# Some key blocks' exponentials moved from ScalarE to VectorE in a two-branch attention kernel

## The chip, the cores and the metric

One NeuronCore of one Trainium2 chip (trn2). The metric is the device time of one execution in microseconds (us), the median over several executions. Runs of one kernel mostly agree within 0.3%. The profile is that of one execution. PE is the matrix engine, PEld its weight loads, ACT is ScalarE, DVE is VectorE, POOL is GpSimd.

## The reference, cut to what matters

```python
def reference(A_x, A_wqkv, A_wo, B_x, B_wqkv, B_wo, gate_w):   # S = 2048 tokens, D = 640, bf16
    x = A_x
    g = sigmoid((x * gate_w).sum(-1, keepdims=True))
    a = A_ref(x, A_wqkv, A_wo)     # full softmax attention, 32 heads of 20
    b = B_ref(x, B_wqkv, B_wo)     # each query sees 8 keys, 2 apart; 32 heads of 20
    return g * a + (1 - g) * b
```

Branch A needs 32 x 2048 x 2048 exponentials. In the kernel that is 2048 *units* of 128 keys x 512 queries (4 query chunks x 8 groups of four heads x 16 key blocks x 4 heads). A *quad* is the four heads of one key block: 4 units.

## The kernel before

The program's order is made when it is built: Python generators ask for tasks, and a small scheduler with a time for each task decides what each engine's queue gets next. ACT computes the exponentials in tiles of 3 and 2 units in turn. PE makes the scores of the next tile, adds the products with the values (`pv`), and does "side" work in what is left: projections, branch B, and the fold (output projection of a finished query chunk). When it has nothing to do it issues filler matmuls that keep it busy. All side work goes through two PSUM banks, `side[0]` and `side[1]`.

```python
mmc = lambda n: max(n, 64) / 2400.0 + 0.004       # the scheduler's times, us
dvc = lambda n, mode=1: 0.10 + n * 1.0417e-3 / mode
actc = lambda n: 0.08 + n * 0.8334e-3

def exp(s):
    u0, n = tiles[s]
    exps[s] = T("act", actc(512 * n), lambda e: e.activation(
        ebuf[s % NE][:, 0:512 * n], score[s % 2][:, 0:512 * n], ACTF.Exp, scale=SCALE),
      reads=[("score", s % 2)], writes=[("ebuf", s % NE)])

def filler(limit):
    while sch.avail["pe"] + 0.32 <= limit and sch.load(2.3) < FILL:
        ...   # a matmul into a free side bank (ident), or into the output bank with zero weights

def gen_fold(qc):                 # output projection of query chunk qc
    while not (done.get(("b", 2 * qc + 1)) and all(done.get(("norm", qc * NQ + q)) for q in range(NQ))):
        yield ("cond",)
    ...                           # 13 accumulating matmuls for each block of 128 tokens

# in the main loop, when a group g of four heads is finished:
if g >= NSLOT:                    # NSLOT output slots, 12 here
    run_until(("fold", (g - NSLOT) // NQ))
```

`gen_bproj` and `gen_b` are branch B: projections and window sums on PE, products on DVE, for 8 blocks of 256 tokens. They and the fold yield `("pe", ...)`, that is, they get PE only where a matmul fits before the next scores are due.

Of the kernel before, what the change touches and what calls it, by code (L numbers as in the profile page):

```python
# [8 lines left out]
U16 = mybir.dt.uint16  # L9
ALU = mybir.AluOpType  # L10
# [18 lines left out]
TOK = 256  # L29

# [195 lines left out]
def _build(ctx, nc, A_x, A_wqkv, A_wo, B_wqkv, B_wo, gate_w, out):  # L226
# [22 lines left out]
    qT = [sb([P, 512], BF16, "qT%d" % i) for i in range(3)]  # L249
    ebuf = [sb([P, 512 * TSZ[i % 2]], BF16, "ebuf%d" % i) for i in range(NE)]  # L250
    NSLOT = 12
    oTn = sb([P, NSLOT, 512], BF16, "oTn")
    oTt = sb([P, 512], FP32, "oTt")
    oNt = sb([P, 512], BF16, "oNt")
# [4 lines left out]
    gB = [sb([P, 512], FP32, "gB%d" % i) for i in range(2)]  # L259
    gwT = sb([P, CN], BF16, "gwT")  # L260
    gwrep = sb([P, CN, P], BF16, "gwrep")
# [15 lines left out]
    repB = [sb([P, 2 * TOK], BF16, "repB%d" % i) for i in range(4)]  # L277
# [7 lines left out]
    Sel = sb([P, 32], BF16, "Sel")  # L285
# [42 lines left out]
    T("dve", 0.06, lambda e: e.memset(warm[:, :], 0.0), writes=["warm"])  # L328
    T("act", 1.4, lambda e: e.activation(warm[:, 2:4], warm[:, 0:2], ACTF.Exp), reads=["warm"], writes=["warm2"])
# [24 lines left out]

    def constants():
# [10 lines left out]
        T("dve", 0.15, lambda e: e.tensor_copy(Sel[:, :], Rep[:, 0:32]), reads=["Rep"], writes=["Sel"])  # L366
# [63 lines left out]
    done = {}  # L430

# [23 lines left out]
    def gen_q(g):  # L455
        qc, q = divmod(g, NQ)
        sl = g % 3
        while not done.get(("k", q)):
# [12 lines left out]
                            mmc(512), first=False)  # L471
        yield ("dve",)
        t = T("dve", dvc(512), lambda e: e.tensor_copy(qT[sl][:, :], side[b][:, :]),  # L473
              reads=[("side", b)], writes=[("qT", sl)])
# [16 lines left out]

    def gen_gate(qc):
        while qc > 1 and not done.get(("fold", qc - 2)):
            yield ("cond",)
        b = yield from bank()
        mms = [(side[b][:, :], gwrep[:, c, :], xT[:, c, qc * 512:(qc + 1) * 512]) for c in range(CN)]
        yield from mm_group(b, mms, ["gwrep"] + XT(qc), mmc(512))
        yield ("act", sch.ready(("side", b)))
        t = T("act", actc(512), lambda e: e.activation(gtan[:, :], side[b][:, :], ACTF.Tanh, scale=0.5),
              reads=[("side", b)], writes=["gtan"])  # L500
        release(b, t)
        yield ("dve",)
        T("dve", dvc(512, 2), lambda e: e.tensor_scalar(gB[qc % 2][:, :], gtan[:, :], -0.5, 0.5, op0=ALU.mult, op1=ALU.add),
          reads=["gtan"], writes=[("gB", qc % 2)])
        yield ("dve",)
        T("dve", dvc(512), lambda e: e.transpose(gtr[:, :], gtan[:, :]), reads=["gtan"], writes=["gtr"])
        T("dve", 0.1, lambda e: e.tensor_scalar(gA[qc % 2][:, :], gtr[:, 0:512:32], 0.5, 0.5, op0=ALU.mult, op1=ALU.add),
          reads=["gtr"], writes=[("gA", qc % 2)])
        done[("gate", qc)] = True

    def gen_norm(g):
# [3 lines left out]
        while not done.get(("gate", qc)):  # L515
# [7 lines left out]
        oo = _ap(oNt, 0, [[32, 16], [1, 32]])  # L523
        ii = _ap(oTt, 0, [[32, 16], [1, 32]])
        T("dve", dvc(512), lambda e: e.tensor_tensor(oo, ii, ib, ALU.mult), reads=["rcp", "oTt"],
          writes=["oNt"])
        yield ("dve",)
        T("dve", dvc(512), lambda e: e.transpose(oTn[:, sl, :], oNt[:, :]), reads=["oNt"],
          writes=[("oTn", sl)])
        done[("norm", g)] = True  # L530

# [10 lines left out]

    def gen_bproj(u):
# [4 lines left out]
        for m in range(3):  # L548
            while m == 2 and u > 0 and not done.get(("bp", u - 1)):
                yield ("cond",)  # L550
            if u > 0 and m > 0:
                bb, key = ((kB, "kB"), (vB, "vB"))[m - 1]
                T("dve", 0.15, lambda e, bb=bb: e.tensor_copy(bb[:, :, 0:PADB], bb[:, :, TOK:TOK + PADB]), reads=[key], writes=[key])
            for f0 in range(0, CN, 2):
# [12 lines left out]
                t = T("dve", dvc(n * TOK), lambda e, o=o, i=i: e.tensor_copy(o, i), reads=[("side", b)], writes=[key])  # L567
# [5 lines left out]
    def gen_b(u):  # L573
        qc, hu = divmod(u, 2)
        while not (done.get(("bqk", u)) and done.get(("gate", qc)) and (u == 0 or done.get(("b", u - 1)))):
            yield ("cond",)

        b = yield from bank()
        for half in range(2):
            for w4 in range(4):  # L580
                w = half * 4 + w4
                yield ("dve",)
                ks = kB[:, :, PADB - DIL * w:PADB - DIL * w + TOK]
                T("dve", dvc(CN * TOK, 2), lambda e, w=w, ks=ks: e.tensor_tensor(prodB(w), qB[:, :, :], ks, ALU.mult),  # L584
                  reads=["qB", "kB"], writes=[("prod", w)] + (["stage"] if u == 0 else []))
            for f in range(CN):
                yield ("pe", 0.11, sch.ready(*[("prod", half * 4 + w4) for w4 in range(4)]))

                def fn(e, f=f, half=half, b=b):
                    ins = None  # L590
                    for w4 in range(4):
                        w = half * 4 + w4
                        pr = _ap(stage, (w * CN + f) * TOK, [[1, TOK]])
                        ins = e.matmul(side[b][32 * w4:32 * w4 + 32, half * TOK:(half + 1) * TOK], Sel[:, :], pr,  # L594
# [4 lines left out]
                T("pe", 0.11, fn, reads=[("prod", half * 4 + w4) for w4 in range(4)] + ["Sel"], mode="col",  # L599
                  **({"writes": [("side", b)]} if (half == 0 and f == 0) else {"accum": [("side", b)]}))  # L600
        done[("bl", u)] = True
        if u == 0:
# [6 lines left out]
        T("dve", dvc(TOK), lambda e, b=b: e.tensor_copy(mB[:, :], side[b][:, 0:TOK]), reads=[("side", b)], writes=["mB"])  # L609
        T("dve", dvc(TOK), lambda e, b=b: e.tensor_tensor(mB[:, :], side[b][:, TOK:2 * TOK], mB[:, :], ALU.max),  # L610
          reads=[("side", b), "mB"], writes=["mB"])
        yield ("dve",)
        T("dve", 0.2, lambda e: e.tensor_copy(cB[0:64, :], mB[64:128, :]), reads=["mB"], writes=["cB"])
        T("dve", 0.25, lambda e: e.tensor_tensor(mB[0:64, :], mB[0:64, :], cB[0:64, :], ALU.max),
          reads=["mB", "cB"], writes=["mB"])
        T("dve", 0.2, lambda e: e.tensor_copy(cB[0:32, :], mB[32:64, :]), reads=["mB"], writes=["cB"])
        T("dve", 0.25, lambda e: e.tensor_tensor(mB[0:32, :], mB[0:32, :], cB[0:32, :], ALU.max),
# [10 lines left out]

        b = yield from bank()
        mms = [(side[b][:, 0:TOK], Rep[:, :], eB[:, hh * TOK:(hh + 1) * TOK]) for hh in range(2)]  # L630
        yield from mm_group(b, mms, ["Rep", "eB"], mmc(TOK), per=2)
        yield ("dve",)
        t = T("dve", TOK * 7.5e-3, lambda e, b=b: e.reciprocal(rB[:, :], side[b][:, 0:TOK]), reads=[("side", b)], writes=["rB"])
        release(b, t)
        T("dve", dvc(TOK), lambda e: e.tensor_tensor(rB[:, :], rB[:, :], gB[qc % 2][:, hu * TOK:(hu + 1) * TOK], ALU.mult),
          reads=["rB", ("gB", qc % 2)], writes=["rB"])
# [3 lines left out]
        for w4 in range(4):  # L640
# [6 lines left out]
            t = T("dve", dvc(512), lambda e, w4=w4, b=b: e.tensor_copy(repB[w4][:, :], side[b][:, :]),  # L647
                  reads=[("side", b)], writes=[("repB", w4)])
            release(b, t)
            for hh in range(2):  # L650
                w = 4 * hh + w4
                yield ("dve",)
                vs = vB[:, :, PADB - DIL * w:PADB - DIL * w + TOK]
                rr = _ap(repB[w4], hh * TOK, [[0, CN], [1, TOK]])
                T("dve", dvc(CN * TOK, 2), lambda e, w=w, vs=vs, rr=rr: e.tensor_tensor(prodB(w), vs, rr, ALU.mult),  # L655
                  reads=["vB", ("repB", w4)], writes=[("prod", w)])
        done[("bp", u)] = True
        for f0 in range(0, CN, 2):
# [9 lines left out]
            t = T("dve", dvc(n * TOK), lambda e, o=o, i0=i0, i1=i1: e.tensor_tensor(o, i0, i1, ALU.mult),  # L668
# [15 lines left out]
    def gen_prefold():  # L684
# [5 lines left out]
        for i in range(3):  # L690
# [9 lines left out]
            release(b, t)  # L700
        for blk in range(2):
# [79 lines left out]
    DVE_AHEAD = 0.9  # L781

    def step(ent, limit, force):
# [7 lines left out]
        elif req[0] == "dve":  # L791
            if not force and sch.avail["dve"] > now + DVE_AHEAD:
                return False
# [29 lines left out]
    def run_until(flag):  # L823
        n = 0
        while not done.get(flag):
            if not any(step(ent, 1e9, True) for ent in list(gens)):
# [84 lines left out]
    t = T("dve", dvc(512), lambda e: e.tensor_copy(qT[0][:, :], side[1][:, :]), reads=[("side", 1)], writes=[("qT", 0)])  # L911
    bank_free[0] = bank_free[1] = t.end + LAT["dve"]
    done[("k", 0)] = done[("q", 0)] = True
    T("dve", 0.5, lambda e: e.tensor_copy(gwrep[:, :, :], _ap(gwT, 0, [[1, CN], [0, P]])), reads=["gwT"], writes=["gwrep"])
# [4 lines left out]
    NU = QCN * NQ * KBN * 4  # L919
    NG = QCN * NQ  # L920
    tiles = []
    u = 0
    while u < NU:
        n = min(TSZ[len(tiles) % 2], NU - u)
        tiles.append((u, n))
        u += n
    NT = len(tiles)
    exps = {}
    tile_of = {}
    for s, (u0, n) in enumerate(tiles):  # L930
        for i in range(n):
            tile_of[u0 + i] = (s, i)

    def qk(s):
        u0, n = tiles[s]
        sc = score[s % 2]

        def fn(e):
            ins = None
            for i in range(n):  # L940
                g, r = divmod(u0 + i, 64)
                kb, j = divmod(r, 4)
                q = g % NQ
                ins = e.matmul(sc[:, i * 512:(i + 1) * 512], kT[32 * j:32 * j + 32, q, kb * P:(kb + 1) * P],  # L944
                               qT[g % 3][32 * j:32 * j + 32, :], start=True, stop=True)
# [3 lines left out]
        for i in range(n):  # L949
            g, r = divmod(u0 + i, 64)  # L950
            rd.add(("kT", g % NQ, r // 16))
            rd.add(("qT", g % 3))
        T("pe", 0.215, fn, reads=sorted(rd, key=str), writes=[("score", s % 2)], mode="row")

    def exp(s):
        u0, n = tiles[s]
        exps[s] = T("act", actc(512 * n), lambda e: e.activation(  # L957
            ebuf[s % NE][:, 0:512 * n], score[s % 2][:, 0:512 * n], ACTF.Exp, scale=SCALE),
          reads=[("score", s % 2)], writes=[("ebuf", s % NE)])

    def pv(units):
        def fn(e):
            ins = None
            for uu in units:
                g, r = divmod(uu, 64)
                kb, j = divmod(r, 4)
                s, i = tile_of[uu]
# [34 lines left out]
    for s in range(NT + 8):  # L1002
        if next_pv >= NU:
            break
# [88 lines left out]
```

## Time and profile before

| | before |
|---|---|
| median time | 974.33 us before the prediction (973.93 with one run more) |
| ACT busy | 945.8 us of 971.4 |
| of it attention exponentials | 930.1 us, 819 tiles, 2048 units: 0.454 us a unit |
| PE busy | 949.5 us, of it fillers 128.1 + 69.1 = 197 us |
| DVE busy | 433.7 us |

The page's first part and its costliest groups. Columns of a group: line, engine, operation, out<-in, shapes, count; busy us, mean ns of one record; idle time before it and who ended it. "+1 forms" means that the group mixes the named shape with one more, and that the mean is over both.

```profile
PE 949.5 (98%) x6989; PEld 326.8 (34%) x6989; DVE 433.7 (45%) x799; ACT 945.8 (97%) x846; POOL 20.3 (2%) x20
...
L957 ACT ACTIVATE ebuf<-score 128x1536 bf16<-128x1536 f32 (+1 forms) x819 | 930.1, 1434 | 5.6 <-PE score L944 5.6
...
L987 PE MATMUL side<-xT,ident 128*128 128x512 bf16 x457 | 128.1, 382 | 0.0
...
L991 PE MATMUL obank<-xT,zero 128*128 128x512 bf16 x232 | 69.1, 383 | 0.0
```

ACT waits 5.6 us for scores in the whole run, so it is the bottleneck. PE only looks as full: the last two lines are fillers. The waits, longest first, say the same from PE's side: it waits for the exponentials.

```profile
PEld score L944 <- ACT ebuf L957: 234.5, 704, 1.2
```

Two groups by form show what a small operand does to one ACT instruction. Both read 512 columns of PSUM; L735 is a plain copy, L870 adds a bias that it reads from a 128x1 tile (`onesrow`).

```profile
L870 ACT ACTIVATE kT<-side,onesrow 128x512 bf16<-128x512 f32 x4 | 2.8, 688 | 6.9 <-DVE kmx L867 5.4 <-PE score L841 1.5
...
L735 ACT ACTIVATE stage<-side 128x512 bf16<-128x512 f32 x2 | 1.1, 594 | 3.9 <-PE side L716 3.9
```

Last, the busy times of 350 to 850 us, the stretch in which branch B and the folds run: all engines, then the two fillers alone.

```profile
350.00:850.00 500.00, 495.52 (x3793) 172.89 (x3791) 237.57 (x422) 500.00 (x448) 0.00 (x0) 1.00 0.02 5
...
350.00:850.00 500.00, 42.88 (x152) 12.37 (x152) 1.00 0.02 5
...
350.00:850.00 500.00, 44.42 (x150) 11.99 (x150) 1.00 0.02 5
```

The columns of the first line are PE, PEld, DVE, ACT, POOL, then clock, DMA share and GB/s; the other two have PE and PEld only. PE's fillers are 42.9 + 44.4 = 87 us of 500 here: 17% of PE is free, while DVE is free for more than half of the stretch.

### The profile page before, as it was taken

How to read it: one execution, taken by the hardware profiler on the slowest of the kernel's cores; microseconds unless marked ns; L12 is line 12 of the kernel's file. 1: busy time of each engine (PE TensorE's matmuls, PEld its weight loads, DVE VectorE, ACT ScalarE, POOL GpSimd, SP SyncE). 2: the span in 40 equal slices, each digit the busy share in tenths (PEclk: the TensorE clock that was granted, in tenths of full speed). 3: DMA queues.
4: the chain of work that ended last, by engine and by line, in shares of the span. 5: the costliest groups of instructions: out<-in, count | busy, mean ns of one | idle time of the engine just before them, and what ended most of it. 6: DMA issues, size and time to landing. Idle time of an engine off the chain costs nothing.

```text
span 971.4 us, 16623 instructions
## 1 busy us (share of the span) xinstructions
PE 949.5 (98%) x6989; PEld 326.8 (34%) x6989; DVE 433.7 (45%) x799; ACT 945.8 (97%) x846; POOL 20.3 (2%) x20
## 2 busy tenths in 40 slices
PE   7989999999999999999999999999999999999997
PEld 4323323223333333333333333334333332333223
DVE  4654434443555722564653364664512556201112
ACT  4989999999999999999999999999999999999996
POOL 0000000007000000000000000000000000000000
PEclk9999999999999999999999999999999999999999
DMA  6110000020000000000000000000000000000000
GB/s 218 26 43 1 1 1 1 13 91 1 1 1 2 1 1 15 15 1 1 1 1 9 20 2 1 1 1 1 2 1 15 14 2 1 1 1 2 1 1 28
DMA packets 9767, 13.05 MB, mean 13 GB/s; under 512 B 2397, under 2 KB 8413, under 8 KB 9693
## 3 DMA queue, kind: packets, MB, share of 16 engines
q1 hardware_dynamic: 9692, 12.00, 3.7%
q8 instruction: 54, 0.88, 0.4%
q14 instruction: 21, 0.16, 0.1%
HBM read 9.38 MB, written 2.62 MB: 12 GB/s over the span
## 4 chain that ended last, share of the span: by engine, by line
PE 61%; ACT 29%; issue 8%; DVE 1%; DMA 0%; DVEq 0%; ACTq 0%
ACT ebuf L957 28%; PE side L420 19%; PE score L944 17%; PE side L987 10%; PE obank L968 10%; PE obank L991 3%; PE side L859 1%; ACT eB L625 1%; PE score L841 1%; DMA oTn<-in_A_x_dram 0%; PE side L643 0%; PE side L594 0%; ACT xT L850 0%; ACT kT L870 0%; PE score L877 0%
## 5 line engine op out<-in xcount | busy, mean ns | idle before, releaser
L957 ACT ACTIVATE ebuf<-score 128x1536 bf16<-128x1536 f32 (+1 forms) x819 | 930.1, 1434 | 5.6 <-PE score L944 5.6
L944 PE MATMUL score<-qT,kT 32*128 32x512 bf16 x2048 | 319.8, 384 | 9.5 <-ACT ebuf L957 4.7
L968 PE MATMUL obank<-ebuf,vA 128*21 128x512 bf16 x2048 | 184.2, 385 | 0.0
L944 PEld LDWEIGHTS score<-qT,kT 32*128 32x128 bf16 x2048 | 78.3, 91 | 256.3 <-ACT ebuf L957 234.5
L420 PE MATMUL side<-xT,kvw 128*128 128x256 bf16 (+1 forms) x740 | 134.8, 295 | 0.0
L987 PE MATMUL side<-xT,ident 128*128 128x512 bf16 x457 | 128.1, 382 | 0.0
L420 PEld LDWEIGHTS side<-xT,kvw 128*128 128x128 bf16 x740 | 59.6, 97 | 58.7 <-issue 42.0
L968 PEld LDWEIGHTS obank<-ebuf,vA 128*21 128x21 bf16 x2048 | 41.6, 89 | 93.4 <-issue 92.1
L991 PE MATMUL obank<-xT,zero 128*128 128x512 bf16 x232 | 69.1, 383 | 0.0
L467 DVE TENSOR_SCALAR qabs<-side 128x512 uint16<-128x512 uint16 x31 | 21.0, 676 | 89.5 <-PE side L420 89.3
L987 PEld LDWEIGHTS side<-xT,ident 128*128 128x128 bf16 x457 | 37.1, 97 | 59.0 <-issue 30.0
L514 DVE STREAM_TRANSPOSE oTt<-obank 128x512 f32<-128x512 f32 x32 | 22.9, 715 | 70.7 <-PE obank L968 70.7
L655 DVE TENSOR_TENSOR stage<-vB,repB 128x1280 bf16<-128x1280 bf16 x64 | 50.1, 822 | 1.1
L584 DVE TENSOR_TENSOR stage<-qB,kB 128x1280 bf16<-128x1280 bf16 x64 | 49.1, 820 | 0.3
L420 PE MATMUL side<-woA_r,oTn 128*128 128x512 bf16 (+1 forms) x248 | 48.2, 302 | 0.0
L420 PE MATMUL side<-stage,ident 128*128 128x512 bf16 (+1 forms) x192 | 48.1, 347 | 0.0
L444 DVE TENSOR_SCALAR kT<-side,onesrow 128x512 bf16<-128x512 f32 x28 | 20.7, 741 | 61.2 <-PE side L420 61.2
L420 PE MATMUL side<-xT,WqP 128*128 128x512 bf16 x155 | 46.6, 384 | 0.8 <-DVE kT L444 0.8
L761 DVE CAST outsb<-side 128x512 bf16<-128x512 f32 (+1 forms) x24 | 11.8, 490 | 75.8 <-PE side L420 75.8
L668 DVE TENSOR_TENSOR oB<-side,rB 128x512 bf16<-128x512 f32 (+1 forms) x24 | 14.5, 603 | 67.7 <-PE side L420 67.7
L420 PE MATMUL side<-woBp,oB 128*128 128x512 bf16 (+1 forms) x160 | 32.5, 302 | 0.0
L473 DVE CAST qT<-side 128x512 bf16<-128x512 f32 x31 | 21.1, 681 | 19.5 <-PE side L420 19.5
(117 smaller groups left out, 500.4 us busy)
## 6 DMA issues: line engine op xcount, KB each, us to landing
stage<-in_B_wqkv_dram SPq DMA_DIRECT2D x1, 2400.0 KB, 8.6
out_dram<-outsb SPq DMA_DIRECT2D x12, 160.0 KB, 1.8
stage<-in_A_wqkv_dram SPq DMA_DIRECT2D x1, 1600.0 KB, 11.0
oTn<-in_A_x_dram SPq DMA_DIRECT2D x2, 640.0 KB, 5.4
kvw<-in_A_wqkv_dram SPq DMA_DIRECT2D x1, 800.0 KB, 8.4
woA_r<-in_A_wo_dram SPq DMA_DIRECT2D x4, 200.0 KB
woBp<-in_B_wo_dram SPq DMA_DIRECT2D x5, 160.0 KB
oB<-in_A_x_dram SPq DMA_DIRECT2D x1, 640.0 KB, 6.9
```

The lines of the kernel that those rows point to most:

```text
L420: ins = e.matmul(o, l, r, start=(first and i == 0), stop=(last and i == n - 1), skip_group_check=True)
L444: t = T("dve", dvc(512), lambda e, b=b, tcc=tcc: e.tensor_scalar(kT[:, q, tcc * 512:(tcc + 1) * 512], side[b][:, :], onesrow[:, 0:1], None ...
L467: T("dve", dvc(512), lambda e: e.tensor_scalar(qabs[:, :].bitcast(U16), side[b][:, :].bitcast(U16)[:, 1:1024:2], 0x7FFF, None, op0=ALU.bit ...
L473: t = T("dve", dvc(512), lambda e: e.tensor_copy(qT[sl][:, :], side[b][:, :]), reads=[("side", b)], writes=[("qT", sl)])
L514: T("dve", dvc(512), lambda e: e.transpose(oTt[:, :], obank[:, :]), reads=["obank"], writes=["oTt"])
L584: T("dve", dvc(CN * TOK, 2), lambda e, w=w, ks=ks: e.tensor_tensor(prodB(w), qB[:, :, :], ks, ALU.mult), reads=["qB", "kB"], writes=[("pro ...
L655: T("dve", dvc(CN * TOK, 2), lambda e, w=w, vs=vs, rr=rr: e.tensor_tensor(prodB(w), vs, rr, ALU.mult), reads=["vB", ("repB", w4)], writes= ...
L944: ins = e.matmul(sc[:, i * 512:(i + 1) * 512], kT[32 * j:32 * j + 32, q, kb * P:(kb + 1) * P], qT[g % 3][32 * j:32 * j + 32, :], start=Tru ...
L957: exps[s] = T("act", actc(512 * n), lambda e: e.activation(ebuf[s % NE][:, 0:512 * n], score[s % 2][:, 0:512 * n], ACTF.Exp, scale=SCALE), ...
L968: ins = e.matmul(obank[32 * j:32 * j + DV, :], vA[:, kb, g % NQ, j, :], ebuf[s % NE][:, i * 512:(i + 1) * 512], start=(kb == 0), stop=(kb ...
L987: t = T("pe", 0.215, lambda e, b=b: e.matmul(side[b][:, :], ident[:, :], xT[:, 0, 0:512], start=True, stop=True), reads=["ident", ("xT", 0 ...
L991: T("pe", 0.215, lambda e: e.matmul(obank[:, :], zero[:, :], xT[:, 0, 0:512], start=False, stop=False, skip_group_check=True), reads=["zer ...
```

## The change

Its intent: ACT is full and VectorE is half idle, so some quads are taken from the end of a group's key blocks and their exponentials are made on VectorE. The queries are scaled by 128/ln 2 and offset so that a score *is*, in effect, the bit pattern of a bf16 power of two; a clamp and a cubic in the fraction then give the exponential in four VectorE passes. The scores of such a unit ride along in a PE row group that a tile's visit leaves free. The gate is computed by block and some buffers are shared, to make room in memory, and the output has 16 slots in place of 12.

```diff
-    qT = [sb([P, 512], BF16, "qT%d" % i) for i in range(3)]
+    qT = [sb([P, 512], BF16, "qT%d" % i) for i in range(2)]
-    NSLOT = 12
+    NSLOT = 16
+    ebias = sb([P, 1], FP32, "ebias")
+    T("dve", 0.06, lambda e: e.memset(ebias[:, :], -127.0 * LN2), writes=["ebias"])
...
-      t = T("dve", dvc(512), lambda e: e.tensor_copy(qT[sl][:, :], side[b][:, :]),
+      t = T("dve", dvc(512), lambda e: e.tensor_scalar(qT[sl][:, :], side[b][:, :], OCT, offs[:, 0:1], op0=ALU.mult, op1=ALU.add),
...
+    def gen_d(w):                       # two of these workers
+        while True:
+            while lock[w] or not wanted():
+                yield ("cond",)
+            b = yield from bank()       # a side bank, until the clamp has read it
+            it = yield ("ride", b)      # scores made beside those of a tile
+            T("dve", dvc(512), ... tensor_scalar(xD[w], side[b], 16384.0, None, op0=ALU.max))
+            release(b, t)
+            nn = xD[w][:, :].bitcast(U16)[:, 0:1024:2]     # the fraction: low half of the fp32 word
+            T("dve", dvc(512), ... scalar_tensor_tensor(tD, nn, -OCT16, nn, op0=ALU.add, op1=ALU.mult))
+            T("dve", dvc(512), ... scalar_tensor_tensor(tD, nn, H1, tD, op0=ALU.add, op1=ALU.mult))
+            T("dve", dvc(512), ... scalar_tensor_tensor(eD as int16, tD, H2, xD[w], op0=ALU.mult, op1=ALU.add))
...
+    BT0 = 230.0
+    BT1 = 910.0
+    BALL = 208.0
+    def d_time():                       # is a new quad allowed?
+        now = sch.avail["pe"]
+        return now >= D0 and sch.avail["dve"] <= now - DIDLE and bdone[0] >= (now - BT0) / (BT1 - BT0) * BALL
...
     def exp(s):
         exps[s] = T("act", actc(512 * n), lambda e: e.activation(
-            ebuf[s % NE][:, 0:512 * n], score[s % 2][:, 0:512 * n], ACTF.Exp, scale=SCALE),
-          reads=[("score", s % 2)], writes=[("ebuf", s % NE)])
+            ebuf[s % NE][:, 0:512 * n], score[s % 2][:, 0:512 * n], ACTF.Exp, scale=LN2 / 128.0, bias=ebias[:, 0:1]),
+          reads=[("score", s % 2), "ebias"], writes=[("ebuf", s % NE)])
```

The tiles that stay on ACT now need a bias, and it is given as a 128x1 tile. And `bdone`, VectorE's work for branch B as the scheduler has booked it, must keep up with a straight line in time, or no new quad is taken. (I call this the pacing rule.)

## The prediction

> **What bounds the kernel now.** ScalarE. The first part of the page has it busy 945.8 of 971.4 us; the groups of instructions give 930.1 us of that to the attention exponentials (819 tiles, 2048 units of 128x512, so 0.454 us a unit). From 100 to 950 us the stretches show it at 50.0 of every 50 us. The waits agree: the weight loads for scores wait 234.5 us for the exponentials, the exponentials only 5.6 us for scores. PE looks 98% busy, but 197 us of it are fillers (128.1 into the side banks, 69.1 into the output bank). VectorE is busy 433.7 us, so some 540 us are free.
>
> **What the change removes.** Each quad (four heads of one key block) moved to VectorE takes 4 x 0.454 = 1.82 us off ScalarE. The scores of these units ride in free row groups, so PE saves a little.
>
> **What it adds on VectorE.** Four full-width passes a unit: one clamp out of PSUM and three dependent fp32 passes. In the trace a 512-wide pass takes 0.69 us; in a row it starts 0.61 us after the one before if independent, and about 0.73 us if it waits for it. That is about 2.8 us a unit, 11 us a quad (estimate). From 100 to 900 us VectorE has about 435 us to spare; one quad is open at a time, banks and the pace kept for branch B cost some of it. I expect 30 quads (24 to 38), 120 units, so ScalarE loses 120 x 0.454 = 54 us. The gate by unit, the slots, the shared buffers move only a few us, off the critical path.
>
> **What it adds on ScalarE, and decides.** The exponential's bias was zero, an immediate; it becomes a 128x1 operand in memory. The Trainium skill ("ScalarE: Activation LUTs", What ACT_TABLE_LOAD costs) says that each such operand adds about 93 ns to an ACTIVATE. The trace agrees for single instructions: copies of 512 columns without one took 594 ns, the key copy with a bias operand 688 ns. In a stream, exponentials now end 1.344 and 0.916 us apart, only 64 ns over their columns' time. Whether the operand's fetch hides there no record shows directly. But one key copy with a bias was followed by a copy whose data were ready, which started 586 ns later, 159 ns over its columns' time, where plain ones start 51 to 67 ns over[...]. So I think it does not hide (62%): 770 tiles x 80 to 93 ns give back 62 to 72 us, more than 30 quads save.
>
> **Time.** Not hidden: 974 - 54 + 65 = 985 with 30 quads, about 970 with 38. Hidden: 974 - 54 = about 920. All of it is on the critical path. I name 968, between the two and nearer the likelier.
>
> **What would show it.** The ends of neighbouring 1536- and 1024-column exponentials: 1.34/0.92 us if hidden, 1.43/1.00 if not. Their number: near 770. VectorE's busy time: near 750 us. Waits of exponentials for scores: still a few us; if tens of us, VectorE or the banks hold PE up. Fillers: fewer than 197 us.
>
> **What would make it wrong.** Far fewer or more quads; strided reads of 16-bit halves slower than 0.69 us a pass; output products that wait for late quads and stall scores behind them on PE; the bias fetch hidden under the tile before (then over 5% faster).
>
> The chances: faster by over 2% 0.40, within 2% 0.50, slower by over 2% 0.10. Predicted 968 us, 908 to 992.

## The result and the profile after

The change gave 1017.52 us (1016.92 to 1017.77, 4 runs) against 973.93 us. A ratio here is the mean time of one kernel's fast runs over that of the other's of the same rounds, so not quite the ratio of the medians quoted: 1.0453, 95% interval 1.0433 to 1.0474. It is 4.5% slower, outside the predicted range. Executions over 1.5% slower than the fastest of the same kernel are left out of the means.

The page's first part and the exponentials of the kernel after:

```profile
PE 922.8 (91%) x6808; PEld 316.5 (31%) x6915; DVE 615.1 (61%) x1067; ACT 985.6 (97%) x827; POOL 22.9 (2%) x20
...
L1135 ACT ACTIVATE ebuf<-score,ebias 128x1536 bf16<-128x1536 f32 (+1 forms) x792 | 971.3, 1592 | 10.8 <-PE score L1121 10.3
```

There are fewer tiles (792 for 819), and they take more time in all (971.3 for 930.1 us). Busy time for a tile went from 930.1/819 = 1.136 us to 971.3/792 = 1.226 us. ACT still waits little for scores, 10.3 us. From start and duration of the records, exponentials of 1536 and 1024 columns ended 1.343 and 0.917 us apart before (medians), 1.431 and 1.004 us after: 87 to 88 ns more each, which is 69 us over 792 tiles.

The four passes of one of the two VectorE workers, by form. The first is the clamp, the last makes the bf16 bits.

```profile
L595 DVE SCALAR_TENSOR_TENSOR eD<-tD,gtan 128x512 int16<-128x512 f32 x36 | 25.9, 718 | 1.0
L592 DVE SCALAR_TENSOR_TENSOR tD<-gtan,tD 128x512 f32<-128x512 uint16 x36 | 25.8, 717 | 0.9
L581 DVE TENSOR_SCALAR gtan<-side 128x512 f32<-128x512 f32 x36 | 24.8, 688 | 11.9 <-PE side L1121 11.1 <-PE side L726 0.5
L589 DVE SCALAR_TENSOR_TENSOR tD<-gtan 128x512 f32<-128x512 uint16 x36 | 24.8, 688 | 1.0
```

They cost what was predicted, 0.69 to 0.72 us each. But the worker did 36 units and the other 32: 68 units, 17 quads, not 30. When they ran shows in the stretches of that last pass (both workers; the columns are DVE busy with the count, clock, DMA share, GB/s):

```profile
100.00:200.00 100.00, 8.28 (x12) 1.00 0.00 1
200.00:300.00 100.00, 12.14 (x15) 0.97 0.07 26
300.00:400.00 100.00, 9.16 (x14) 1.00 0.00 1
400.00:500.00 100.00, 5.44 (x8) 1.00 0.02 8
500.00:600.00 100.00, 2.06 (x3) 1.00 0.00 1
600.00:700.00 100.00, 3.45 (x5) 1.00 0.02 8
700.00:800.00 100.00, 2.75 (x4) 1.00 0.00 1
800.00:900.00 100.00, 0.00 (x0) 1.00 0.02 8
900.00:1016.00 116.00, 5.53 (x8) 1.00 0.02 7
```

About ten quads (41 units) fall before 400 us and about five after 500 us. VectorE had time left: from 350 to 850 us it was busy 280.5 of 500 us. (The trace of this run lacks 107 matmul records, 6808 for 6915 weight loads, so its PE times come out a little low.)

So there are two questions. Is the longer tile really the bias operand? And what kept the quads at 17?

### The profile page after: what moved, and what is told of

Read it like the earlier page. It is cut to its first block, busy times and chain, and to the rows that moved or that the text cites. A ratio compares the mean times of both kernels' runs of the same rounds, so it can differ in the third digit from the quotient of the medians.

```text
span 1016.0 us, 16619 instructions
## 1 busy us (share of the span) xinstructions
PE 922.8 (91%) x6808; PEld 316.5 (31%) x6915; DVE 615.1 (61%) x1067; ACT 985.6 (97%) x827; POOL 22.9 (2%) x20
## 4 chain that ended last, share of the span: by engine, by line
ACT 68%; issue 21%; PE 7%; DVE 3%; DMA 1%; DVEq 0%; ACTq 0%
ACT ebuf L1135 67%; PE score L1121 2%; PE side L445 2%; PE obank L1165 1%; ACT tB L713 1%; DMA oTn<-in_A_x_dram 1%; PE side L948 0%; DVE qT L503 0%; PE score L930 0%; DVE eD L595 0%; ACT eB L701 0%; DVE oTt L560 0%; DVE tD L592 0%; DVE oTt L549 0%; DVE oTn L563 0%
## 5 line engine op out<-in xcount | busy, mean ns | idle before, releaser
L1135 ACT ACTIVATE ebuf<-score,ebias 128x1536 bf16<-128x1536 f32 (+1 forms) x792 | 971.3, 1592 | 10.8 <-PE score L1121 10.3
L1121 PE MATMUL score<-qT,kT 32*128 32x512 bf16 x1980 | 308.5, 385 | 70.4 <-ACT ebuf L1135 39.7
L1165 PE MATMUL obank<-ebuf,vA 128*21 128x512 bf16 x1980 | 178.2, 386 | 1.1 <-ACT ebuf L1135 1.1
L1183 PE MATMUL obank<-xT,zero 128*128 128x512 bf16 x379 | 113.8, 383 | 2.9 <-issue 2.4
L1183 PEld LDWEIGHTS obank<-xT,zero 128*128 128x128 bf16 x423 | 33.6, 97 | 53.8 <-issue 37.3
L445 PE MATMUL side<-woA_r,oTn 128*128 128x128 bf16 (+1 forms) x242 | 45.5, 299 | 0.4 <-issue 0.3
L1179 PE MATMUL side<-xT,ident 128*128 128x512 bf16 x145 | 43.6, 381 | 0.7 <-issue 0.5
L751 DVE SCALAR_TENSOR_TENSOR oB<-side,rB 128x512 bf16<-128x512 f32 (+1 forms) x24 | 14.4, 600 | 42.1 <-PE side L445 40.4
L503 DVE TENSOR_SCALAR qT<-side,offs 128x512 bf16<-128x512 f32 x31 | 23.1, 744 | 21.7 <-PE side L445 20.7
L716 DVE RECIPROCAL rB<-side 128x256 f32<-128x256 f32 x8 | 14.1, 1758 | 31.6 <-ACT tB L713 31.6
```

The source lines that it names most:

```text
L445: ins = e.matmul(o, l, r, start=(first and i == 0), stop=(last and i == n - 1), skip_group_check=True)
L503: t = T("dve", dvc(512), lambda e: e.tensor_scalar(qT[sl][:, :], side[b][:, :], OCT, offs[:, 0:1], op0=ALU.mult, op1=ALU.add), reads=[("si ...
L1121: ins = e.matmul(o, kT[32 * j:32 * j + 32, q, kb * P:(kb + 1) * P], qT[g % 2][32 * j:32 * j + 32, :], start=True, stop=True)
L1135: exps[s] = T("act", actc(512 * n), lambda e: e.activation(ebuf[s % NE][:, 0:512 * n], score[s % 2][:, 0:512 * n], ACTF.Exp, scale=LN2 / 1 ...
L1165: ins = e.matmul(obank[32 * j:32 * j + DV, :], vA[:, kb, g % NQ, j, :], src, start=(kb == 0), stop=(last and k >= len(lst) - 4), skip_grou ...
L1179: t = T("pe", 0.215, lambda e, b=b: e.matmul(side[b][:, :], ident[:, :], xT[:, 0, 0:512], start=True, stop=True), reads=["ident", ("xT", 0 ...
```

## The experiments

Theory A: the operand is fetched in the open, once for each ACTIVATE, also in a stream of them. Rival B: VectorE's new passes slow ACT's tiles down through shared memory. For the second question, the prediction's theory was that VectorE's spare time limits the quads; the rival, formed after the result, is that PE's left-over slots for branch B do, by way of the pacing rule. Nine kernels ran.

### The bias and the quads, each alone

Four kernels make a square with the change: with and without the operand, with and without quads.

`e1_imm`, the change with the bias as an immediate:

```diff
-  ... ACTF.Exp, scale=LN2 / 128.0, bias=ebias[:, 0:1]), reads=[("score", s % 2), "ebias"], ...
+  ... ACTF.Exp, scale=LN2 / 128.0, bias=-127.0 * LN2), reads=[("score", s % 2)], ...
```

> The changed kernel with the exponential's bias as an immediate, every engine's order the same. Theory A (the 128x1 bias operand is fetched in the open, 87 ns a tile): exponentials end 1.34 and 0.92 us apart again, 792 x 0.087 = 69 us less than the change, about 948 us, 2.5 to 3% faster than before. Rival B (the tiles are slower because VectorE's new passes share memory with ScalarE): spacing stays 1.43 and 1.00 us, about 1017 us.

`e2_before_ptr`, the kernel before with an operand of zeros:

```diff
+    T("dve", 0.06, lambda e: e.memset(ebias[:, :], 0.0), writes=["ebias"])
-  ... ACTF.Exp, scale=SCALE), reads=[("score", s % 2)], ...
+  ... ACTF.Exp, scale=SCALE, bias=ebias[:, 0:1]), reads=[("score", s % 2), "ebias"], ...
```

> The kernel before with a 128x1 operand of zeros as the exponential's bias, nothing else. A: 819 x 0.087 = 71 us more, about 1045 us, spacing 1.43 and 1.00 us. B: as before, 974 us.

`e3_noquad_imm`, the change with the immediate and no quad at all:

```diff
-    D0 = 100.0
+    D0 = 1e9          # no quad before this time; and the immediate bias of e1_imm
```

> The changed kernel without any quad on VectorE and with the immediate bias: what the gate by unit, the 16 slots and the shared buffers cost by themselves. A: within 5 us of before, 972 to 980 us. If they cost more (a rival for part of the loss): over 985 us.

`e4_noquad_ptr`, the same with the operand kept:

> The changed kernel without any quad, bias operand kept. A: about 1047 us, so the 17 quads (68 units x 0.454 to 0.49 us) save 30 us whichever the bias. B: near 976 us, as no pass on VectorE is left.

Measured (medians of 4 runs; before 972.73 us in the same rounds; the time of the change is that of its own rounds, where before took 973.93 us):

| | immediate bias | 128x1 operand | the operand costs |
|---|---|---|---|
| kernel before | 972.73 | 1045.62 (e2_before_ptr) | 72.9 |
| change, no quads | 976.35 (e3_noquad_imm) | 1047.47 (e4_noquad_ptr) | 71.1 |
| change, 17 quads | 952.23 (e1_imm) | 1017.52 (the change) | 65.3 |

All four results were right. Theory A holds and B falls: the operand alone makes the kernel before 7.5% slower (ratio 1.0749), with no new work on VectorE, and without the operand the change is 2.1% faster than before (ratio 0.979, interval 0.9774 to 0.9806). That is clear of no gain, but the interval crosses the 2% line, so the verdict on record is "unclear", and it is less than the 2.5 to 3% expected. The tiles of `e2_before_ptr`, then those of `e1_imm`:

```profile
L959 ACT ACTIVATE ebuf<-score,ebias 128x1536 bf16<-128x1536 f32 (+1 forms) x819 | 1003.1, 1616 | 5.3 <-PE score L946 5.3
```

```profile
L1135 ACT ACTIVATE ebuf<-score 128x1536 bf16<-128x1536 f32 (+1 forms) x792 | 901.6, 1411 | 14.4 <-PE score L1121 13.4
```

(1003.1 - 930.1)/819 = 89 ns a tile more with the operand, (971.3 - 901.6)/792 = 88 ns less without it; the ends lie 1.432 and 1.005 us apart in the first, 1.343 and 0.917 us in the second. In `e1_imm` each engine's instructions stand in the same order as in the change; the operand is the only difference. What is shown is that the 88 ns belong to the operand and stay in a stream; that they are the time of a fetch is the theory's name for them, and no run shows it.

The rest of the change (gate, slots, shared buffers) costs 976.35 - 972.73 = 3.6 us. The 17 quads save 24.1 us with the immediate and 30.0 us with the operand, where 68 x 0.454 = 30.9 us was the most to expect with the immediate. Most of the missing 7 us may be in the waits: `e1_imm` waits 13.4 us for scores, `e3_noquad_imm` 7.1.

### What limits the quads

The number of quads is fixed when the program is built, by the times that its scheduler books, so it can be read from the build without the chip: the expectations below name it beforehand, and every trace had just that number. The runs show whether the plan holds on the chip and what it gains.

The next four kernels all have the immediate bias. `e5_nopace` switches the pacing rule off:

```diff
-    BALL = 208.0
+    BALL = 0.0
```

> Immediate bias; the rule that holds quads back while branch B is behind is switched off, and the kernel's own scheduler then places 40 quads. The prediction's theory (only VectorE's spare time limits the quads): 40 x 4 x 0.454 = 73 us below the version without quads, about 903 us. Rival (branch B needs PE slots, banks and VectorE that the quads take; it ends late and the rest of it runs after the attention): well over 976 us, some 1050 us, with the exponentials waiting for scores for tens of us.

It took 1083.34 us (2 runs), with a right result; ratio 1.1129. It did place 40 quads (160 units in the trace), and ACT's busy time fell to 876.6 us. But ACT then waits, as its waits after 500 us show (us in total, times, longest):

```profile
ACT eB L701 <- PE side L698: 71.6, 2, 37.5
ACT ebuf L1135 <- PE score L1121: 64.3, 4, 38.0
ACT stage L820 <- PE side L801: 34.2, 1, 34.2
```

The exponentials end at 968 us; then branch B and the folds run alone for over 100 us. Before that, attention stops twice for long (ACT is busy 26.1 of the 40 us from 520 us and 16.0 of the 40 us from 760 us); in the program's order it may be only 16 groups ahead of a fold (`NSLOT`), and the fold waits for branch B. So quads do delay branch B, and the pacing rule is needed. The prediction's theory of this run, 903 us, fails.

`e6_lightPE` keeps the rule and takes away most of branch B's and the folds' matmuls. Its output is wrong, which doesn't matter for the time. VectorE's work for branch B stays whole.

```diff
-    mms += [(side[b]..., oTn[...], woA_r[...]) for q in range(NQ)]          # fold: 13 steps
+    mms = mms[:1]                                                           # 1 step
-    ... xT[:, c, t0:t0 + TOK]) for c in range(CN)]                          # B's projections: 5 steps
+    ... xT[:, c, t0:t0 + TOK]) for c in range(1)]
-    for w in (0, 4, 1, 5, 2, 6, 3, 7)]                                      # B's window sum
+    for w in (0, 4)]
```

> Immediate bias, pacing rule kept; most of branch B's and of the output projection's matmuls left out (one of five steps of B's projections, two of eight windows of its sum, one of thirteen of the fold; wrong result on purpose), VectorE's work unchanged. The scheduler places 29 quads in place of 17. If PE's left-over slots hold the quads back: 12 x 1.82 = 22 us less than the first experiment, about 930 us. If VectorE does: it cannot carry 12 more quads without exponentials waiting, and the time stays near 950 us.

`e7_noquad_lightPE` is its control: the same cuts, no quads.

> Control for the light-PE run: the same matmuls left out, no quad. Both theories: those matmuls are not on the critical path themselves, so 976 us within 4 us. If it falls by 10 us or more, the light-PE gain is not due to quads.

Measured: 932.63 us with quads (ratio 0.958), 975.57 us without (ratio 1.002). The cuts alone gain nothing (976.35 us without them), and with quads they gain 952.23 - 932.63 = 19.6 us, near the 22 us of 12 more quads. The trace shows 116 units, 29 quads. So VectorE could carry 29 quads; in 17 it was not at its limit. The stretch of 350 to 850 us, first in `e1_imm`, then in `e6_lightPE` (columns as before):

```profile
350.00:850.00 500.00, 496.52 (x3867) 174.72 (x3866) 296.91 (x513) 500.00 (x454) 0.00 (x0) 1.00 0.02 5
```

```profile
350.00:850.00 500.00, 475.68 (x3540) 149.25 (x3602) 416.53 (x704) 500.00 (x454) 0.00 (x0) 1.00 0.02 5
```

VectorE goes from 297 to 417 us of 500, with ACT full in both. This run does not separate PE's time from the two side banks: fewer matmuls also hold a bank for less time.

The fillers of `e1_imm` in the same stretch bear on that (PE and PEld; first those into the side banks, then those into the output bank):

```profile
350.00:850.00 500.00, 13.98 (x41) 3.79 (x41) 1.00 0.02 5
...
350.00:850.00 500.00, 66.23 (x225) 17.55 (x225) 1.00 0.02 5
```

They take 80 us in all, against 87 us before the change, so the quads hardly used PE's free time. But `filler` goes to the output bank only when the scheduler has no side bank free, and these rose from 44.4 to 66.2 us while those into the side banks fell from 42.9 to 14.0. This speaks for the side banks as the scarce thing and against PE's time; no run changes the banks alone, so it is not shown.

`e8_twopass` tries the other side. It leaves out the two middle passes of each unit (the cubic), so that only the clamp and the conversion are left, a straight line between powers of two:

```diff
-    T("dve", ... tD = (nn - OCT16) * nn)
-    T("dve", ... tD = (nn + H1) * tD)
-    T("dve", ... scalar_tensor_tensor(eD as int16, tD, H2, xD[w], op0=ALU.mult, op1=ALU.add))
+    T("dve", ... scalar_tensor_tensor(eD as int16, xD[w], 0.0, xD[w], op0=ALU.mult, op1=ALU.add))
```

> Immediate bias, pacing kept, two of the four VectorE passes of a unit left out (wrong result on purpose), PE's work whole. The scheduler places 24 quads. If VectorE's passes are a second limit beside PE's slots: 7 x 1.82 = 13 us less than the first experiment, about 939 us. If PE's slots alone limit: no gain, 950 us.

It took 939.36 us (ratio 0.9647) with 24 quads, as expected. So the passes are a limit too. Whether it is the time that they take from branch B on VectorE, or the length of a quad's chain of passes (only one quad is open at a time), this run does not tell. It passed the comparison with the reference: the few blocks treated this way tolerate the straight line at this tolerance. It is a coarser approximation all the same, and I do not offer it as the better kernel.

### A version that beats both

`e9_tuned` is right and keeps the cubic. It has the immediate bias, one worker in place of two, so that quads hold at most one of the two side banks, and other constants of the rule:

```diff
+    (immediate bias of e1_imm)
-    add_gen(gen_d(1), 1.01)
-    D0 = 100.0; DTIME = 15.0; DIDLE = -1.0; DAHEAD = 0.5; BT0 = 230.0
+    D0 = 60.0;  DTIME = 17.0; DIDLE = -0.5; DAHEAD = 0.3; BT0 = 250.0
```

> Immediate bias, whole cubic, right result: only one quad worker in place of two (at most one side bank held by quads) and other constants of the pacing rule, with which the scheduler places 25 quads. If quads that leave branch B its banks and slots are worth their 1.82 us each: 8 x 1.82 = 15 us less than the first experiment, about 938 us, 3.6% faster than before. If the extra quads push B late, as without the rule: 950 us or more.

It took 937.88 us (937.66 to 939.40, 4 runs) against 973.04 us: ratio 0.9645, interval 0.9628 to 0.9662, 3.6% faster than the kernel before. It places 25 quads, eight more than the change, without pushing branch B late, and with none of PE's work left out. Its worker and its constants were changed together, so which of them made room for the eight is not shown.

```profile
PE 901.4 (96%) x6865; PEld 311.4 (33%) x6865; DVE 693.1 (74%) x1195; ACT 902.0 (96%) x814; POOL 23.4 (2%) x20
```

## Why the prediction was wrong

It said 968 us, 908 to 992; the time was 1017.52 us. Point by point:

- **ACT is the bottleneck: right.** Its waits for scores stayed small (10.3 us), and what its tiles cost came out in the time.
- **The bias operand does not hide: right, in kind and size.** The prediction gave 80 to 93 ns a tile; 87 to 88 ns were measured, and the square of runs puts it at 65 to 73 us of the time. The evidence had been in the trace before: the 688 ns copy against the 594 ns one, and the copy that started 159 ns late. The prediction only gave it a chance of 62% and named a time between the two outcomes. That was one part of the error: in its own case "not hidden" it had 985 us.
- **"I expect 30 quads (24 to 38)": wrong, and this is the step that failed.** There were 17. It was worked out from VectorE's spare time alone ("VectorE has about 435 us to spare"). Banks and pace were mentioned, but not costed. The cost of a quad was right: VectorE's busy time rose by (615.1 - 433.7)/17 = 10.7 us a quad, where 11 were predicted. The count was not: the runs showed that the pacing rule stops the quads while VectorE has time left, because branch B must keep up and attention may not run far ahead of it. With most of the matmuls of branch B and the folds cut, 29 quads fitted (e6_lightPE); with half of the passes, 24 (e8_twopass); with one worker and other constants, 25 (e9_tuned); with the rule off, 40, and 1083 us (e5_nopace). Which of side banks, passes and PE's slots holds branch B back first stays open.
- **PE's free time, read from the total of its fillers: not shown to have failed.** "PE looks 98% busy, but 197 us of it are fillers" is true of the run. In the stretch where branch B runs, 350 to 850 us, only 87 of 500 us were. But with 17 quads 80 us of fillers were still there (e1_imm), and with 25 quads 63.8 + 12.1 = 76 us (e9_tuned), so the quads did not run out of PE time in total.
- **The sum with the right count.** 974 - 68 x 0.454 + 792 x 0.088 + 3.6 = 974 - 31 + 70 + 4, about 1016 us before rounding. With the count mended, the operand in the open and the 3.6 us of the rest, the prediction's own sum comes within about 1 us of the measured time.
- **VectorE busy "near 750 us", "near 770" tiles:** 615.1 us and 792, both from the count. A pass at 0.69 us, fillers fewer than 197 us (113.8 + 43.6 = 157 in the groups) and few waits for scores: right.
- **The chance of "slower by over 2%", 0.10, was too small.** The change without quads took 1047.47 us (e4_noquad_ptr), and a quad saved 30.0/17 = 1.76 us. To come within 2% (under 974 x 1.02 = 993.5 us) it would have taken 54/1.76, about 31 quads; so even the expected 30 left no room, and the range of counts was too narrow on the low side.

Why did the change come out slower although its quads do save time? Its scheduler books `actc(512 * n)`, 0.08 us and 0.8334 ns a column, for both forms of the exponential. To it the operand was free. Its quads saved 30 us of the 71 us that the operand cost.

## What to carry to other kernels

When a change adds an operand to the one instruction that fills the bottleneck engine, cost it for each instruction and multiply by the count before looking at what the change removes; try an immediate first. When work is moved to an idle engine, read the other resources that it shares (matrix slots, PSUM banks) in the stretch where it will run, not as a total over the run. Where the program's builder decides how much work moves, build it and count, instead of estimating the count. A scheduler inside a kernel is a cost model: check that it books the changed instruction's new time.

## What the Trainium skill lacked or had wrong

- "ScalarE: Activation LUTs", What ACT_TABLE_LOAD costs: it states that each 128x1 operand adds about 93 ns to an ACTIVATE and that neighbours in a row overlap by about 93 ns. It does not say whether the operand's part remains in a row. These runs: 87 to 88 ns of it remain (ends 1.343 to 1.431 us and 0.917 to 1.004 us apart), 65 to 73 us of a kernel of 819 or 792 such tiles.
- The same section gives 186 ns + 0.833 ns a column for an ACTIVATE with an immediate, and does not name the memory that it reads. It fits the one here that reads SBUF: 2240 columns in 2052 ns, 186 ns over its columns. The copy of 512 columns from PSUM took 594 ns, which is 167 ns over its columns, and in a row an exponential from PSUM cost 63 ns over its columns.
- The same section's overlap of about 93 ns comes out roughly here if the tile alone is the measure: in the kernel before, the two tiles of 1024 columns that started on an idle engine took 1024 and 1025 ns, and in a row such tiles ended 917 ns apart (median), some 108 ns less. The mean record in a row is longer, 1221 ns; the section does not say so, and 1221 - 917 = 304 ns is not the overlap that it means. In a row, the distance of the ends is the cost, not the duration of a record.
- "VectorE: DVE Perf Modes", the perf-mode tier table, has no row for scalar_tensor_tensor. A pass over 512 columns, with a 16-bit source at a stride of two elements, took 688 to 717 ns here, next to 691 ns for 512 columns of the fp32 tensor_tensor that the page gives in its section on the TRN2 errata: the stride cost nothing that shows.
